# Down tiles of a SwiGLU beside attention: two steps in one group, and two PSUM banks as one tile

## The chip, the cores and the metric

The kernel runs on one core of a Trainium2 chip. The metric is the device time of one execution, in microseconds: the median of three runs of the kernel before is 1884.03 us (1881.98 to 1886.42). PE is TensorE, DVE VectorE, ACT ScalarE, POOL GpSimd, SP the queue that issues most DMAs.

## The reference

One transformer block on 2048 rows of width 512, in float32. There are 32 heads of 16 columns. The feed-forward width is 1792.

```
mod = silu(c) @ w_mod                      # shift, scale, gate, twice
h = layernorm(x) * (1 + ca) + sa
q, k, v = split(h @ wqkv);  p = softmax(q k^T / 4);  x = x + ga * ((p v) @ wo)
h = layernorm(x) * (1 + cb) + sb
x = x + gb * ((silu(h @ w_gate) * (h @ w_up)) @ w_down)
```

## The kernel before, in words

Float32 operands are split into a high part and a low part, and a product is three matmuls (high-high, high-low, low-high). Queries come in 4 chunks of 512 columns, heads in 8 groups of four, so attention is 32 units of 16 key tiles: 512 **steps**. A step is four **pairs**, one for each head of the group. One pair (`pair_of`, line 895) is

- a score matmul S (`score`, L506) with 50 of the 128 rows, and the exponential of its bank on ACT (L508);
- a max matmul M (`max_one`, L479) with 48 rows, of a step 20 steps ahead, and the row maximum of its bank on DVE (L481).

S and M sit in opposite row halves of the PE array and run at the same time. Every 16 steps `max_rows` adds three small matmuls (L491 to L493). PV matmuls (`pv_step`, L521) use all 128 rows and 32 columns each, and come in **halves**; each half is four matmuls in the program and eight records in the trace. They stand between runs of pairs.

PSUM has eight banks, and before the change each is a tile of its own. The order on PE is written out by hand in two kinds of stage:

- `plain` (line 928): **windows** of three pairs, then one or two PV halves (2, 1, 1, 2 in turn). M takes banks 0, 1, 2, 3 in turn, S takes 4, 5, 6 in turn. So every fourth M uses bank 3 and every third S uses bank 6. The row maximum sums in `max_rows` also take one turn of S's banks, so that after each 16 steps the bank 6 falls on another place in the window.
- `filled` (line 941): one **group** of two steps (`TWO`) or one step (`ONE`), with other matmuls put between its pairs (the numbers in the tuple say how many steps of that work follow each pair), and then its PV halves. M uses banks 0 to 2, S banks 4 and 5, and the work put in accumulates in banks 3 and 6 (`FBANKS`). The work is the output projection, the gate and up products (24 steps of two matmuls, in two `TWO` groups) or a **down tile** pair (12 steps of two matmuls, in two `ONE` groups).

The work put in goes through `accumulate` (line 709) in two **phases**: in phase 0 bank 3 sums products of rows 0 to 63 and bank 6 those of rows 64 to 127; in phase 1 they trade row halves. Before the change the two phases of a down tile lie in two groups, with PV matmuls of all 128 rows between them. After phase 1 DVE adds both banks to `x2` (L791).

After the last pair (about 1718 us) nothing is left of attention but its end, and `whole` runs the remaining 35 jobs on pairs of banks (0,1), (2,3), (4,5), (6,7) in turn, with all 128 rows (L727). Before the first pair, in the prologue, projections (L209) take banks 4 to 6, and the first 80 M take banks 0 to 3 beside them.

A matmul, a reduce or an exponential that needs a tile waits on the semaphore of the engine that used it last; the recording layer puts these waits in, tile by tile.

Of the kernel before, what the change touches and what calls it, by code (L numbers as in the profile page):

```python
# [9 lines left out]
F32 = mybir.dt.float32  # L10
# [9 lines left out]
P = 128  # L20
# [8 lines left out]
CW = S // NC  # L29
NG = H // 4  # L30
NU = NG * NC
NF = F // P
FG = 2
# [11 lines left out]
FBANKS = (3, 6)  # L45
# [2 lines left out]
NORM = 9  # L48
STARTS = (147, 275, 403)
TWO = (0, 3, 2, 2, 2, 2, 1, 0)  # L50
ONE = (0, 3, 3, 0)
ALONE = {TWO: ((0, 4, 0, 4, 0, 4, 0, 0), (4, 5, 0, 1, 5, 0, 4, 1)), ONE: ((0, 6, 0, 0), (4, 5, 4, 0))}


def run(it):
    for _ in it:
        pass


def take(it, k):  # L60
    run(islice(it, k))
# [40 lines left out]
def block_kernel(ctx, tc, x, wqkv, wo, w_gate, w_up, w_down, c, w_mod, out):  # L102
    nc = tc.nc
# [5 lines left out]
    ps = ctx.enter_context(tc.tile_pool(name="ps", bufs=1, space=PSUM))  # L109
    sm = Stream()  # L110

    banks = [ps.tile([P, CW], F32, name=f"bank{i}") for i in range(8)]

    class Turn:
        def __init__(self, *ids):
# [6 lines left out]
    four, bank, single = Turn(0, 1, 2, 3), Turn(4, 5, 6), Turn(7)  # L122
# [326 lines left out]
    pb = ctx.enter_context(tc.tile_pool(name="pb", bufs=2, reuse_waits="tile"))  # L449
# [7 lines left out]
    def ones_rows(k):  # L457
        for b in range(2):
            rows = slice(64 * b + KR, 64 * b + KR + 2)
            nc.sync.dma_start(kop[k][rows].bitcast(F32), kop[0][rows].bitcast(F32))  # L460

    def load_k(u):
        load_parts(kop[u % 3], kd, u % NG, 0, S, nc.gpsimd if u > 2 else nc.sync)

    def load_q(u):
        ci, g = divmod(u, NG)
        qop[u] = pb.tile([P, 2, CW], F32R, name="qop", tag="qop", bufs=3)
        load_parts(qop[u], qd, g, ci * CW, (ci + 1) * CW, nc.gpsimd if u > 2 else nc.sync)
# [14 lines left out]
    def max_rows(u):  # L483

        m = pb.tile([P, 16], F32, name="m", tag="m")
        nc.vector.tensor_reduce(m, mx.pop(u).rearrange("p b s t f -> p (b s t) f"), op=ALU.max, axis=AX.X)
        nm = pb.tile([P, 16], F32R, name="nm", tag="nm")

        def rows():
            pr = bank("pr")[0:16, 0:2 * P]  # L490
            nc.tensor.matmul(pr[:, 0:P], nm.bitcast(F32), ident, start=True, stop=True)  # L491
            nc.tensor.matmul(pr[:, P:2 * P], m, minus, start=True, stop=False)  # L492
            nc.tensor.matmul(pr[:, P:2 * P], nm.bitcast(F32), minus, start=False, stop=True)  # L493
            mr = pb.tile([16, 2, P], F32R, name="mr", tag="mr", bufs=1)
            nc.scalar.copy(mr, pr.rearrange("p (r q) -> p r q", r=2))
            for r in range(2):
                nc.sync.dma_start(qop[u][KR + r:KR + r + 65:64].bitcast(F32), mr[:, r, :].bitcast(F32))
        side.extend([lambda: None, lambda: None, lambda: nc.scalar.mul(nm, m, -1.0), lambda: None, rows])
# [207 lines left out]
            nc.gpsimd.tensor_copy(self.hT[0][:, k, :], h32)  # L706
            eng.tensor_sub(self.hT[1][:, k, :], h32, self.hT[0][:, k, :].bitcast(F32))

    def accumulate(outs, lhs, rhs, nk, after, halves, by_k=False):

        terms = [(k, a, b) for k in range(nk) for a, b in ((0, 0), (0, 1), (1, 0))]
        z = len(terms) - 1
        if halves:
            for ph in range(2):
                for j, (k, a, b) in enumerate(terms):
                    for e in range(2):
                        rows = slice(64 * (ph ^ e), 64 * (ph ^ e) + 64)
                        nc.tensor.matmul(outs[e], lhs(e, a, k)[rows], rhs(b, k)[rows],  # L718
                                         start=(ph == 0 and j == 0), stop=(ph == 1 and j == z))
                    if ph == 1 and j == z:  # L720
                        after()
                    yield
        else:
            order = [(e, j) for e in range(2) for j in range(z + 1)]
            for e, j in sorted(order, key=lambda o: o[1] // 3) if by_k else order:
                k, a, b = terms[j]
                nc.tensor.matmul(outs[e], lhs(e, a, k), rhs(b, k), start=(j == 0), stop=(j == z))  # L727
                if e == 1 and j == z:
                    after()
                yield  # L730
# [21 lines left out]
    def out_pair(ch, t0, outs, halves):  # L752
        return accumulate(outs, lambda e, a, k: ch.oT[a][:, k, (t0 + e) * P:(t0 + e + 1) * P],
                          lambda b, k: ch.wo[k // 2][:, b, k % 2, :], NK,
                          lambda: posts.append(lambda: add_o(ch, t0, outs, True)), halves)
# [31 lines left out]
    def down(ch, m, t0, outs, halves):  # L787
        def later():
            for e in range(2):
                t = t0 + e  # L790
                nc.vector.tensor_add(ch.x2[:, t, :], outs[e], ch.x2[:, t, :])  # L791
                if m == NF // FG - 1:
                    (nc.sync if ch.ci == last else nc.gpsimd).dma_start(od[:, 4 * ch.ci + t, :], ch.x2[:, t, :])

        def after():
            if halves:
                later()
            else:
                posts.append(later)
            if t0:  # L800
                ch.load_wd(m + 1)

        mids, wd = [ch.mid[FG * m + k] for k in range(FG)], ch.wd[m]
        return accumulate(outs, lambda e, a, k: mids[k][:, a, (t0 + e) * P:(t0 + e + 1) * P],
                          lambda b, k: wd[:, b, k, :], FG, after, halves, m == NF // FG - 1)

    chunks = {}
    side = []

    def begin(ci):  # L810
        x2 = pf.tile([P, 4, D], F32, name="x2", tag="x2", bufs=1)
        act = [pf.tile([P, NK, CW], F32R, name=f"act{a}", tag=f"act{a}", bufs=1) for a in range(2)]
        hT = [pf.tile([P, NK, CW], F32R, name=f"act{a}", tag=f"act{a}", bufs=1) for a in range(2)]
        chunks[ci] = ch = Chunk(ci, x2, act, hT)
        ch.load_x2(nc.sync if ci else nc.gpsimd)
# [8 lines left out]
    def hook():  # L824
        while posts:
            posts.pop(0)()
# [34 lines left out]
    def after(i):  # L861
        nonlocal pf
        for f in due.pop(i, []):
            f()
        j = i + LEAD
        if j % 16 == 15 and j < n:
            max_rows(j // 16)
        if i == -2:
            run(late)
            sm.finish()  # L870
            es_a0.close()
            pf = ctx.enter_context(tc.tile_pool(name="pf", bufs=1, side="right", reuse_waits="tile"))
            kop[2] = pf.tile([P, 2, S], F32R, name="kop2")
            ones_rows(2)
            load_k(2)
            load_q(2)
        if 0 <= i < UG and i % 16 in (3, 5, 8):
            next(weights2, None)
# [12 lines left out]
    halves = [(i, half) for i in range(n) for half in range(2)]  # L891
# [3 lines left out]
    def pair_of():  # L895
        nonlocal done
        i = done // 4 - 1
        most = 4 * n - 4 * (LEAD - 1)
        score(i + 1, (ORDER if done < most else (0, 1, 2, 3))[done % 4])
        if done < most:  # L900
            max_one(done + 4 * (LEAD - 1))
        done += 1
        if side:
            side.pop(0)()
# [17 lines left out]
    def end_steps():  # L922
        nonlocal ended
        while ended < done // 4:
            after(ended - 1)
            ended += 1
# [14 lines left out]
    def filled(places, work):  # L941

        nonlocal four, bank
        four, bank = three, Turn(4, 5)
        if done >= 4 * n - 4 * (LEAD - 1):
            places, order = ALONE.get(places, (places, (4, 5, 0, 1)))
            bank = Turn(*order)
        for r in range(len(places)):
            pair_of()
            take(work, places[r])  # L950
            if r % 4 == 3:
                end_steps()
        hook()
        pvs(6, False)
# [12 lines left out]
    outs = [banks[b] for b in FBANKS]  # L967
    for ci in range(last):
        plain(STARTS[ci] - done // 4)
        ch = chunks[ci]  # L970
        for t0 in (0, 2):
            work = out_pair(ch, t0, outs, True)
            filled(TWO, work)
            filled(TWO, work)
        side.append(lambda: scaled(ch))
        plain(NORM)
        plain(WIN, [lambda tp, k=k: ch.turned(tp, k) for k in range(NK)])
        if ci == last - 1:
            plain(REST)
        for _ in range(len(ch.jobs) - (KEEP if ci == last - 1 else 0)):  # L980
            job, args = ch.jobs.pop(0)
            if args == (NF // FG - 1, 0):
                plain(WIN)
            work = job(ch, *args, outs, True)
            for _ in range(2):
                filled(TWO if job is gate_up else ONE, work)
    chunks[last - 1].load_gu(NF - 2)
    filled((0,) * 4, iter(()))

# [70 lines left out]
```

## Time and profile before

| | |
|---|---|
| median of 3 runs | 1884.03 us |
| profiled execution: time, span | 1885.85 us, 1884.0 us |
| mean granted TensorE clock | 0.998 |
| PE, DVE, ACT, POOL busy | 99%, 82%, 66%, 22% of the span |
| chain of waits that ended last | PE 93%, DVE 3%, ACT 2%, DMA 2% |
| S and M | 2048 each (L506, L479), and as many exponentials and maxima |
| matmuls of the filled work | L718: 1872 + 288 of gate, up and output, 912 of down |

How to read it: a group row gives line, engine, operation, tiles and shapes, then the busy time, the mean ns of one, and the idle time of the engine before it. A row of the timeline begins with start and duration. A row of the windows view gives the stretch, its length, and the busy time of PE, PEld (weight loads), DVE, ACT and POOL with their counts. Bank numbers are left out of tile names. PE records overlap, since two row halves work at once, so PE's busy share says little of how full it is.

### The profile page before, as it was taken

The page shows a single profiled execution, that of the slowest core. Times are in us where ns is not written, and L with a number is a line of the kernel's source. Part 1 is how long each engine was busy: PE and PEld are TensorE (multiplying, and loading weights), DVE is VectorE, ACT ScalarE, POOL GpSimd, SP SyncE. Part 2 cuts the span into 40 slices and gives each one's busy share as a digit, 9 for nine tenths or more (in the row PEclk, how much of TensorE's full clock was granted, in tenths as well). Part 3 has the DMA queues.
Part 4 walks back from the last instruction along what each step waited for, and adds up shares of the span by engine and source line. Part 5 has one row for each costly group of instructions (what it writes and reads, how often), then busy time and mean ns, then how long its engine had stood idle before and what let it go on. Part 6 is the DMA issues. An engine that isn't in the chain of part 4 may idle for free.

```text
span 1884.0 us, 40835 instructions
## 1 busy us (share of the span) xinstructions
PE 1857.0 (99%) x16996; PEld 1145.3 (61%) x16996; DVE 1537.1 (82%) x2558; ACT 1249.8 (66%) x2330; POOL 414.6 (22%) x498
## 2 busy tenths in 40 slices
PE   7999999999999999999999999999999999999999
PEld 5766444444455666666555666666454566666887
DVE  5458999999999888888999888888999988831643
ACT  4221888888887766667777666667778866774211
POOL 3000554455323111111123111111123011031200
PEclk9999999999999999999999999999999999999999
DMA  8764777667843543554454453453643445243642
GB/s 297 279 213 124 178 182 196 181 172 184 209 85 78 140 110 117 141 128 88 112 118 114 105 137 116 127 121 78 153 91 55 102 98 128 107 160 122 243 184 109
DMA packets 78852, 267.60 MB, mean 142 GB/s; under 512 B 17364, under 2 KB 22484, under 8 KB 57988
## 3 DMA queue, kind: packets, MB, share of 16 engines
q1 hardware_dynamic: 59820, 180.10, 32.9%
q0 software_dynamic: 18160, 84.10, 19.0%
q8 instruction: 133, 2.18, 0.5%
q10 hardware_dynamic: 688, 0.80, 0.1%
q14 instruction: 51, 0.42, 0.1%
HBM read 201.85 MB, written 62.13 MB: 140 GB/s over the span
## 4 chain that ended last, share of the span: by engine, by line
PE 93%; DVE 3%; ACT 2%; DMA 2%; issue 0%; SPq 0%; ACTq 0%; DVEq 0%
PE bank L521 26%; PE bank L506 23%; PE bank L718 19%; PE bank L479 10%; PE bank L209 7%; PE bank L727 6%; DVE mx L481 1%; PE bank L491 1%; DVE stt L743 1%; PE bank L162 0%; PE bank L703 0%; DMA wm_ab<-in_w_mod 0%; PE bank L493 0%; PE bank L492 0%; PE bank L279 0%
## 5 line engine op out<-in xcount | busy, mean ns | idle before, releaser
L481 DVE TENSOR_REDUCE mx<-bank 128x1 f32<-128x512 f32 x2048 | 1282.9, 682 | 134.5 <-PE bank L479 86.5
L479 PE MATMUL bank<-kop,qop 48*128 48x512 f32 x2048 | 757.6, 434 | 3.3 <-DVE mx L481 3.1
L506 PE MATMUL bank<-qop,kop 50*128 50x512 f32 x2048 | 748.0, 429 | 3.3 <-DMA qop<-mr 0.5
L506 PEld LDWEIGHTS bank<-qop,kop 50*128 50x128 f32 x2048 | 344.5, 185 | 312.1 <-issue 48.1
L479 PEld LDWEIGHTS bank<-kop,qop 48*128 48x128 f32 x2048 | 342.4, 184 | 30.8 <-DVE mx L481 13.9
L718 PE MATMUL bank<-act,wgu 64*128 64x512 f32 x1872 | 296.6, 393 | 0.0
L718 PEld LDWEIGHTS bank<-act,wgu 64*128 64x128 f32 x1872 | 186.2, 187 | 31.4 <-issue 0.2
L548 POOL TENSOR_TENSOR on<-o,rb 128x512 f32<-128x512 f32 x31 | 39.7, 1281 | 450.7 <-DMA rb<-d_dr 299.1
L718 PE MATMUL bank<-wd,mid 64*128 64x512 f32 x912 | 130.8, 392 | 0.0
L779 POOL CAST mid<-m 128x512 fp32r<-128x512 f32 x40 | 24.3, 607 | 428.4 <-PE bank L479 175.4
L718 PEld LDWEIGHTS bank<-wd,mid 64*128 64x128 f32 x912 | 89.2, 186 | 15.2 <-issue 0.7
L209 PE MATMUL bank<-hT,wqs 128*128 128x512 f32 x384 | 95.8, 399 | 2.3 <-ACT hT L328 1.0
L209 PEld LDWEIGHTS bank<-hT,wqs 128*128 128x128 f32 x384 | 70.3, 188 | 24.4 <-issue 6.1
L775 DVE SCALAR_TENSOR_TENSOR q<-th,bank 128x512 f32<-128x512 f32 x56 | 37.7, 673 | 56.8 <-ACT th L771 56.8
L771 ACT ACTIVATE th<-bank 128x512 f32<-128x512 f32 x56 | 33.2, 594 | 58.5 <-PE bank L727 58.4
L791 DVE TENSOR_TENSOR x<-bank,x 128x512 f32<-128x512 f32 x84 | 53.9, 685 | 19.6 <-PE bank L718 19.6
L369 DVE TENSOR_TENSOR prt<-bank,prt 128x512 fp32r<-128x512 f32 x32 | 22.0, 688 | 46.2 <-ACT prt L367 43.9
L367 ACT CAST prt<-bank 128x512 fp32r<-128x512 f32 x32 | 18.8, 586 | 59.1 <-PE bank L209 47.1
L777 DVE TENSOR_TENSOR m<-bank,q 128x512 f32<-128x512 f32 x56 | 38.7, 691 | 21.2 <-PE bank L727 19.2
L727 PE MATMUL bank<-wd,mid 128*128 128x512 f32 x216 | 52.3, 395 | 0.5 <-DVE mid L780 0.3
L780 POOL TENSOR_TENSOR mid<-m,mid 128x512 fp32r<-128x512 f32 x40 | 51.6, 1289 | 3.3
L718 PE MATMUL bank<-wgu,act 64*128 64x512 f32 x288 | 47.7, 395 | 0.1
(6281 smaller groups left out, 5144.0 us busy)
## 6 DMA issues: line engine op xcount, KB each, us to landing
wgu<-gu_dr SPq DMA_DIRECT2D x48, 1024.0 KB
wd<-wd_dr SPq DMA_DIRECT2D x28, 1024.0 KB
kop<-kd SPq DMA_DIRECT2D x33, 768.0 KB
kop<-kd POOLq DMA_DIRECT2D x29, 768.0 KB, 8.5
gu_dr<-wgu POOLq DMA_DIRECT2D x14, 1024.0 KB, 14.3
kd<-prt SPq DMA_DIRECT2D x16, 512.0 KB
qd<-prt SPq DMA_DIRECT2D x16, 512.0 KB
kop<-gu_dr SPq DMA_DIRECT2D x8, 1024.0 KB
```

Of the source, the lines that this page charges most:

```text
L209: nc.tensor.matmul(pt, lhs(a, k), rhs(b, k), start=(n == 0), stop=(n == 3 * nk - 1))
L479: nc.tensor.matmul(pm, qop[u][rows, s, qt * P:(qt + 1) * P], kop[u % 3][rows, s, kc * CW:(kc + 1) * CW], start=True, stop=True)
L481: nc.vector.tensor_reduce(mx[u][:, b, s, qt, kc:kc + 1], pm, op=ALU.max, axis=AX.X)
L506: nc.tensor.matmul(sp, kop[u % 3][rows, h // 2, kt * P:(kt + 1) * P], qop[u][rows, h // 2, :], start=True, stop=True)
L521: nc.tensor.matmul(pv[u][32 * h:32 * h + 32, cols], v_flat[:, e0:e0 + 32], p_[h][:, cols], start=(kt == 0 and half == 0), stop=(kt == 15), ...
L548: mul.tensor_mul(on, o, rb)
L718: nc.tensor.matmul(outs[e], lhs(e, a, k)[rows], rhs(b, k)[rows], start=(ph == 0 and j == 0), stop=(ph == 1 and j == z))
L727: nc.tensor.matmul(outs[e], lhs(e, a, k), rhs(b, k), start=(j == 0), stop=(j == z))
L775: nc.vector.scalar_tensor_tensor(q, th, 1.0, outs[0], op0=ALU.add, op1=ALU.mult)
L777: nc.vector.tensor_mul(m32, outs[1], q)
L780: (nc.gpsimd if slow else nc.vector).tensor_sub(mid[:, 1, :], m32, mid[:, 0, :].bitcast(F32))
L791: nc.vector.tensor_add(ch.x2[:, t, :], outs[e], ch.x2[:, t, :])
```

## The change

Three things are changed.

1. `ONE`, a group of one step with three filled steps after pairs 1 and 2, is replaced by `DOWN`, a group of two steps: phase 0 after pairs 1 and 2, phase 1 after pairs 4 and 5, nothing after pairs 6 and 7. A down tile has one group now, and so one run of four PV halves in place of two runs of two. The table for the stage without M (`ALONE`) is changed to match.
2. Between the phases there are no PV matmuls any more. Instead ACT copies one element of both banks into a small tile `first` (`trade`), behind the last matmuls of phase 0, and the first matmul of phase 1 waits for that read.
3. To be read by one instruction, banks 3 and 6 become one tile `fpair` of two banks, and `banks[3]` and `banks[6]` are its two halves. All other users of these banks go through this tile too.

```diff
-ONE = (0, 3, 3, 0)
-ALONE = {TWO: ((0, 4, 0, 4, 0, 4, 0, 0), (4, 5, 0, 1, 5, 0, 4, 1)), ONE: ((0, 6, 0, 0), (4, 5, 4, 0))}
+DOWN = (0, 3, 3, 0, 3, 3, 0, 0)
+ALONE = {TWO: (0, 4, 0, 4, 0, 4, 0, 0), DOWN: (0, 6, 0, 0, 0, 6, 0, 0)}
...
-    banks = [ps.tile([P, CW], F32, name=f"bank{i}") for i in range(8)]
+    fpair = ps.tile([P, 2, CW], F32, name="fpair")
+    banks = [fpair[:, FBANKS.index(i), :] if i in FBANKS else ps.tile([P, CW], F32, name=f"bank{i}") for i in range(8)]
...
-    def accumulate(outs, lhs, rhs, nk, after, halves, by_k=False):
+    def accumulate(outs, lhs, rhs, nk, after, halves, by_k=False, trade=None):
...
-                                         start=(ph == 0 and j == 0), stop=(ph == 1 and j == z))
-                    if ph == 1 and j == z:
-                        after()
+                                         start=(ph == 0 and j == 0), stop=(j == z and (ph == 1 or trade is not None)),
+                                         skip_group_check=(ph == 1 and trade is not None))
+                    if j == z:
+                        (after if ph else trade or (lambda: None))()
...
-                          lambda b, k: wd[:, b, k, :], FG, after, halves, m == NF // FG - 1)
+                          lambda b, k: wd[:, b, k, :], FG, after, halves, m == NF // FG - 1,
+                          lambda: nc.scalar.copy(first[:, :, None], fpair[0:1, :, 0:1]))
...
+    first = pb.tile([1, 2], F32, name="first", bufs=1)
...
-            places, order = ALONE.get(places, (places, (4, 5, 0, 1)))
-            bank = Turn(*order)
+            places, bank = ALONE.get(places, places), Turn(4, 5, 0, 1, 5, 0, 4, 1)
...
-            for _ in range(2):
-                filled(TWO if job is gate_up else ONE, work)
+            for places in (TWO, TWO) if job is gate_up else (DOWN,):
+                filled(places, work)
```

**PE in a plain window.** The rows are in program order, with the engine whose semaphore each waits for; the lines are one higher after the change. In the names before, bank_63 to bank_70 are banks 0 to 7. After it fpair stands for banks 3 and 6, and bank_64, 65, 66, 67, 68, 69 are banks 0, 1, 2, 4, 5, 7. Before:

```order
L506 MATMUL bank_68<-qop,kop_961 128x512 [waits Activation_49]
L479 MATMUL bank_65<-kop_87,qop 128x512 [waits DMAHW7_49,DMAHW0_49,DVE_49]
L506 MATMUL bank_69<-qop,kop_961 128x512 [waits Activation_49]
L479 MATMUL bank_66<-kop_87,qop 128x512 [waits DVE_49]
L506 MATMUL bank_67<-qop,kop_961 128x512 [waits Activation_49]
L479 MATMUL bank_63<-kop_87,qop 128x512 [waits DVE_49]
L521 MATMUL bank_70<-pt__3750,v_flat 32x256
```

and the same place now:

```order
L507 MATMUL bank_68<-qop,kop_960 128x512 [waits Activation_49]
L480 MATMUL bank_66<-kop_86,qop 128x512 [waits DMAHW7_49,DMAHW0_49]
L507 MATMUL fpair<-qop,kop_960 128x512 [waits Activation_49]
L480 MATMUL fpair<-kop_86,qop 128x512 [waits Activation_49]
L507 MATMUL bank_67<-qop,kop_960 128x512
L480 MATMUL bank_64<-kop_86,qop 128x512 [waits DVE_49]
L522 MATMUL bank_69<-pt__3750,v_flat 32x256
```

No instruction moved here. The M on bank 3 (fourth row) waited for DVE and now waits for ACT; the count that it waits for is that of the exponential of the score in the row above it. In the window before this one stand an M and an S on fpair behind each other:

```order
L507 MATMUL bank_68<-qop,kop_960 128x512 [waits Activation_49]
L480 MATMUL fpair<-kop_1425,qop 128x512 [waits Activation_49]
L507 MATMUL fpair<-qop,kop_960 128x512 [waits DVE_49]
L480 MATMUL bank_64<-kop_86,qop 128x512 [waits DMASW3_49,DMASW2_49]
L507 MATMUL bank_67<-qop,kop_960 128x512 [waits Activation_49]
L480 MATMUL bank_65<-kop_86,qop 128x512
```

The S on bank 6, which waited for ACT before, waits for DVE here, and the count is that of the maximum of the M in the row above it. By the counts of the whole program, M on bank 3 waits in 78 cases for the exponential of its own pair, in 85 for that of the pair before and in 77 for that of two pairs before; S on bank 6 waits in 82 cases for the maximum of the pair before, in 77 for that of two and in 76 for that of three pairs before. Before the change there is not one such wait: M waited for the maximum four pairs back and S for the exponential three pairs back.

**PE in a down tile**, at the start of phase 1. Before, with the last three of the eight PV rows that stand between the phases:

```order
L521 MATMUL bank_70<-pt__8831,v_flat 32x256
L521 MATMUL bank_70<-pt__8822,v_flat 32x256
L521 MATMUL bank_70<-pt__8840,v_flat 32x256
L506 MATMUL bank_67<-qop,kop_961 128x512 [waits Activation_49]
L479 MATMUL bank_63<-kop_1425,qop 128x512 [waits DVE_49]
L506 MATMUL bank_68<-qop,kop_961 128x512 [waits Activation_49]
L479 MATMUL bank_64<-kop_1425,qop 128x512 [waits DVE_49]
L718 MATMUL bank_66<-wd,mid 128x512
```

and now, from the end of phase 0:

```order
L720 MATMUL fpair<-wd,mid 128x512
L507 MATMUL bank_68<-qop,kop_960 128x512 [waits Activation_49]
L480 MATMUL bank_66<-kop_1425,qop 128x512 [waits DVE_49]
L507 MATMUL bank_67<-qop,kop_960 128x512 [waits Activation_49]
L480 MATMUL bank_64<-kop_1425,qop 128x512 [waits DVE_49]
L720 MATMUL fpair<-wd,mid 128x512 [waits Activation_49]
L720 MATMUL fpair<-wd,mid 128x512 x5
L507 MATMUL bank_68<-qop,kop_960 128x512 [waits Activation_49]
```

The PV rows have left the middle of the tile, two pairs stand between the phases, and the first matmul of phase 1 waits for ACT, for the small copy. On ACT that copy stands between the exponentials of pairs 2 and 3:

```order
L509 ACTIVATE pt__8846<-bank_68 128x512 [waits PE_49]
L509 ACTIVATE pt__8875<-bank_67 128x512 [waits PE_49]
L509 ACTIVATE pt__8880<-bank_68 128x512 [waits PE_49]
L509 ACTIVATE pt__8891<-bank_67 128x512 [waits PE_49]
L809 COPY first<-fpair 1x2 [waits PE_49]
L509 ACTIVATE pt__8903<-bank_68 128x512 [waits PE_49]
```

Those are 38 new instructions on ACT, one for each down tile beside attention.

## The prediction

> **What bounds the kernel now.** I read the page's busy times first, then the windows view for the plain stages, then the timeline of single windows.
>
> ```profile
> PE 1857.0 (99%) x16996; PEld 1145.3 (61%) x16996; DVE 1537.1 (82%) x2558; ACT 1249.8 (66%) x2330; POOL 414.6 (22%) x498
> 192.00:546.50 354.50, 353.78 (x3532) 165.55 (x3524) 350.61 (x597) 307.31 (x606) 168.72 (x172) 1.00 0.69 178
> 404.55:411.70 7.15, 7.15 (x76) 3.36 (x72) 7.15 (x13) 6.19 (x12) 0.00 (x0) 1.00 0.96 345
> ```
>
> The first line makes PE the bound of the whole. The second is the longest plain stretch: there DVE is busy for 350.61 of 354.50 us, too. The third is one cycle of it, 12 pairs in four windows: 7.15 us, and DVE has no idle time in it. So a plain cycle costs 7.15 us, set by DVE, with PE's own work just beneath:
>
> ```profile
> 404.18 4.26 DVE L481 TENSOR_REDUCE mx<-bank 128x1 f32<-128x512 f32 x7
> 404.55 0.49 PE L506 MATMUL bank<-qop,kop 50*128 50x512 f32 x1
> 404.88 0.39 PE L506 MATMUL bank<-qop,kop 50*128 50x512 f32 x1
> 405.08 0.60 ACT L508 ACTIVATE pt__4169<-bank 128x512 f32<-128x512 f32 x1 [0.63 <-PE bank L479]
> 405.12 0.39 PE L506 MATMUL bank<-qop,kop 50*128 50x512 f32 x1
> 405.57 0.59 ACT L508 ACTIVATE pt__4174<-bank 128x512 f32<-128x512 f32 x1
> 406.05 0.61 ACT L508 ACTIVATE pt__4179<-bank 128x512 f32<-128x512 f32 x1
> 406.44 0.50 PE L506 MATMUL bank<-qop,kop 50*128 50x512 f32 x1
> 407.90 0.50 PE L506 MATMUL bank<-qop,kop 50*128 50x512 f32 x1
> ```
>
> In a window the three scores start at 0, 0.33 and 0.57 us (404.55, 404.88, 405.12). The next window starts 1.89 us after the first score with two PV halves (406.44) and 1.46 us with one (407.90). A cycle has two of each: 2 x 1.89 + 2 x 1.46 = 6.70 us of PE alone. The exponentials start 0.53, 1.02 and 1.50 us after the window's first score, since each follows the one before by 0.49. A maximum takes 4.26/7 = 0.61 in a row of seven; I use 0.60.
>
> **The change, first part: one tile for banks 3 and 6.** No instruction of a plain window moves, but M on bank 3 now waits for an exponential on bank 6, and S on bank 6 for a maximum on bank 3 (the waits of the built program, shown with the change). Such a wait stood nowhere before, so its price comes from single links of the chain where the engines were idle:
>
> ```profile
> 651.26 0.50 PE L506 MATMUL bank<-qop,kop 50*128 50x512 f32 x1
> 651.26 0.73 PE L479 MATMUL bank<-kop,qop 48*128 48x512 f32 x2
> 651.80 0.60 ACT L508 ACTIVATE pt__7287<-bank 128x512 f32<-128x512 f32 x1 [1.22 <-PE bank L506]
> 651.83 1.89 DVE L481 TENSOR_REDUCE mx<-bank 128x1 f32<-128x512 f32 x3 [0.18 <-PE bank L506]
> 652.45 0.18 PEld L506 LDWEIGHTS bank<-qop,kop 50*128 50x128 f32 x1 [0.19 <-ACT pt__7287 L508]
> 652.53 0.42 PE L506 MATMUL bank<-qop,kop 50*128 50x512 f32 x1
> ```
>
> An exponential ends at 652.40 and the matmul that waited for it starts at 652.53: 0.13. So a matmul that waits for the exponential of a window's first score can start 0.53 + 0.60 + 0.13 = 1.26 after that score, for the second score's 1.75 and for the third's 2.24. A maximum starts 0.57 after its M (651.26 to 651.83) and takes 0.68 (1.89 for three, pitch 0.60); with 0.10 for the release a waiting score starts 1.35 after a window's first M, and 1.95 if it is the second in DVE's queue. PE takes its matmuls in order, so all that stands behind the held one waits with it: the window's other pairs, its PV halves, and behind them ACT and DVE run empty.
>
> Number the pairs of a cycle 0 to 11; M on bank 3 is in pairs 3, 7 and 11. S on bank 6 stands on the first, second or third place of every window (the place moves by one each 16 steps). The holds are the price less the time at which PE would have come there by itself:
>
> - first place (pairs 0, 3, 6, 9): M3 waits for its own pair, 1.26; M7 for pair 6, 1.26 - 0.33 = 0.93; M11 for pair 9, 1.26 - 0.57 = 0.69; S of the next pair 0 for M11's maximum, 1.35 - (1.46 - 0.57) = 0.46. Sum 3.34.
> - second place: M3 for pair 1, over one PV half, 1.75 - 1.46 = 0.29; S4 for M3's maximum, 1.35 - 0.33 = 1.02; M7 for its own pair, 1.75 - 0.33 = 1.42; M11 for pair 10, 1.75 - 0.57 = 1.18. Sum 3.91.
> - third place: M3 for pair 2, 2.24 - 1.46 = 0.78; S5 for M3, 1.35 - 0.57 = 0.78; S8 for M7, 1.95 - 0.57 = 1.38; M11 for its own pair, 2.24 - 0.57 = 1.67. Sum 4.61.
>
> The mean is 3.95 on PE's own 6.70: 10.65 us a cycle, where DVE's 7.15 hid 0.45 of it: **+3.50**. Bounds: without any queue on ACT and DVE (every price 1.26 or 1.35, in-window holds alone) the places give 2.88, 3.11 and 3.06, mean 3.0, so 9.7 and +2.55; if all cycles were like the third place, 11.31 and +4.16. How many cycles: 240 M wait for ACT (78 + 85 + 77), three to a cycle, so 80. The page gives nearly the same:
>
> ```profile
> L718 PE MATMUL bank<-act,wgu 64*128 64x512 f32 x1872 | 296.6, 393 | 0.0
> L718 PE MATMUL bank<-wd,mid 64*128 64x512 f32 x912 | 130.8, 392 | 0.0
> L718 PE MATMUL bank<-wgu,act 64*128 64x512 f32 x288 | 47.7, 395 | 0.1
> ```
>
> (1872 + 288)/48 = 45 jobs of 16 pairs and 912/24 = 38 down tiles of 8 leave 2048 - 720 - 304 - 4 = 1020 pairs to plain windows, 85 cycles. I take 80: 80 x 3.50 = **+280 us**, between 80 x 2.55 = 204 and 85 x 4.16 = 354.
>
> The same tile joins the two banks in the prologue and the tail:
>
> ```profile
> 145.00:192.00 47.00, 45.72 (x205) 29.09 (x207) 41.57 (x69) 10.82 (x21) 3.18 (x4) 1.00 0.43 120
> L727 PE MATMUL bank<-wd,mid 128*128 128x512 f32 x216 | 52.3, 395 | 0.5 <-DVE mid L780 0.3
> L791 DVE TENSOR_TENSOR v_flat<-bank,v_flat 128x512 f32<-128x512 f32 x28 | 19.3, 689 | 10.6 <-PE bank L727 10.2
> ```
>
> In the prologue ten projection matmuls on bank 6 now wait for the fourth of four maxima in a row, up to 0.57 + 3 x 0.60 + 0.68 + 0.10 = 3.15 after the first M, of which the four M hide about 0.9. That is 22 us at most; DVE is idle for 5.4 of 47 us there, so part of the hold is work that DVE owes anyway. I take +12, bounds 3 and 22. In the tail a job on banks 6 and 7 follows one on 2 and 3 seven times, and must wait for the last add from bank 3: matmul 0.40, add 0.69, two releases 0.2, less a pitch of 0.2, so 1.1 each: +7, bounds 0 and 12. The small matmuls of `max_rows` no longer lie in DVE's shadow in plain stages: 0 to 14, I take +5.
>
> **Second part: one group in place of two.**
>
> ```profile
> 654.82:658.39 3.57, 3.57 (x42) 2.16 (x38) 3.00 (x5) 2.28 (x4) 0.00 (x0) 1.00 0.11 17
> 806.10:812.88 6.78, 6.78 (x78) 4.66 (x74) 5.65 (x9) 4.57 (x8) 3.04 (x4) 1.00 0.77 209
> L498 ACT ACTIVATE nm<-m x32: 207/216/232, 175.4 to 1660.9; 128x16 fp32r<-128x16 f32 x32
> ```
>
> The first stretch is a one-step group of a down tile with its PV run, the second a two-step group of a gate and up tile: it has just twice the matmuls of each kind. 2 x 3.57 - 6.78 = 0.36 is the price of one more passage between row halves and PV. 38 tiles x 0.36 = **-13.7**. DVE has 9 operations in the second stretch, 5.65 us; a down tile gives it ten (8 maxima, 2 adds), some 6.3, so it fits into 6.78.
>
> The trade costs ACT one small copy, nearest row 0.22. It starts when phase 0's last matmul has ended, 0.40 + 0.05 after its start; add 0.22 and 0.13, and phase 1 can start 0.80 after that matmul. Two pairs stand between, at the 0.24 of the window above (404.88 to 405.12), so PE comes there after 0.72: 0.08 a tile, 3 us for 38. Behind the copy ACT has the exponential of pair 3, which only the score of pair 5 needs. The bounds are 0 and 0.35, if the copy queues behind half an exponential (13 us): I take +3. Together -11, between -14 and 0. The cover of the copy is those two pairs; without them it would cost 0.80 - 0.24 = 0.56 a tile, 21 us.
>
> **Sum**: 280 + 12 + 7 + 5 - 11 = +293 on the profiled span of 1884.0 us: 2177. That execution took 1885.85, 1.85 more than its span, and the median of the three runs is 1884.03, as good as the span; I forecast **2177 us**. The bounds added are 1884 + 204 + 3 - 14 = 2077 and 1884 + 354 + 22 + 12 + 14 + 0 = 2286, all unlikely at once.
>
> **The rivals.**
>
> *The new waits stand on work that has ended* (not slower). Then the plain cycle stays at 7.15 and only the second part is left: 1884 - 11 = **1873**. For it speaks that holds over two PV halves are nil in my list, since 1.26 is less than 1.89. Against it: the M that waits for its own pair's exponential cannot be early, as that exponential starts 0.53 after the score beside it. It decides from the point where the prices fall below the gap of 0 to 0.6 us; no row shows an exponential that short. The Trainium skill, page "PSUM — Partial Sum Buffer", section "Specifications (TRN2)", says that ScalarE and VectorE can read PSUM in parallel at full bandwidth as long as there is no bank collision. By that rule banks 3 and 6 need no order between them, and the chip would give the 1873; the rows of the built program have the waits all the same. Chance 0.05.
>
> *One hold a cycle*: a hold lets ACT and DVE catch up, and the others vanish in its shadow. Then a cycle is 6.70 + 1.45 (mean of 1.26, 1.42 and 1.67) = 8.15, +1.0 x 80: with the other terms **1977**. Against it: each hold is measured from a score or M that itself comes after the earlier hold. Chance 0.07.
>
> *The granted clock falls* where PE stops three or four times in 10 us. It is 1.00 in the windows rows above. At half clock PE's own 6.70 would double at most, +536; over half the plain time **2445**. Against it: no hold is longer than 1.7 us. Chance 0.05. The skill's page "TensorE: Matmul & The Clock Gate", section "A second HAM failure mode: psum-queue depth-cycling", tells of a kernel that cycled through PSUM banks, with micro-idle times between groups of matmuls, and whose clock swung between half and full. No run here shows that yet.
>
> **How the numbers follow.** My forecast has 0.83, the rivals 0.05, 0.07 and 0.05. The likeliest case's own range is 2090 to 2250: the two bounds drawn in, since its terms do not all err one way. It holds most of the 0.83, and what is left out is about 2 in 10, so it is the range. 0.2% of 1884 is 3.8 us, which is what a measurement can tell from no change; only the first rival could be faster (0.04) or the same (0.02, with a dearer trade). Slower 0.94.
>
> **What would show it.** Right: in the same plain stretch a cycle of 10 to 11.5 us, DVE some 67% busy in it (7.15 of 10.65), PE's idle time before L480 released by the exponentials (L509) and before L507 by the maxima (L481), some 235 times each, in the first case 1.2 to 1.7 long for M of the own pair; down tiles at 6.7 to 6.9 us a group; clock still 1.00. Wrong: a plain cycle of 7.2, or holds before L480 of 0.3 and less; a clock below 1; or 38 long waits on the small copy (L809).

## The result, and the profile after

The changed kernel takes **2429.26 us** in the median (six runs, 2421.35 to 2471.52), the kernel before 1884.68 us in the runs beside it: a ratio of **1.288** (95% interval 1.285 to 1.291; the medians themselves give 1.289). The forecast was 2177 us, range 2090 to 2250: the direction was right, and 252 us are missing. The profiled execution of the changed kernel is its slowest, 2471.52 us at a mean clock of 0.837, where the other five have 0.854 to 0.867, so its stages are read below by clock, and the ratios here and below leave out executions more than 1.5% above the fastest of the same kernel.

From the page of the changed kernel, the busy times, the granted clock in 40 slices, and the chain of waits by engine:

```profile
PE 2225.3 (90%) x16996; PEld 1254.6 (51%) x16996; DVE 1589.2 (64%) x2558; ACT 1280.4 (52%) x2368; POOL 415.0 (17%) x498
PEclk9987559675765797999995989999857768999999
PE 83%; DVE 8%; ACT 8%; issue 1%; DMA 0%; SPq 0%; ACTq 0%; DVEq 0%
```

DVE fell from 82% to 64% of a longer span, and DVE and ACT entered the chain with 8% each, from 3% and 2%. That is the theory of holds. But the second line was not foreseen: the clock, 1.00 before, goes down to half for whole slices. The windows view of the changed kernel (columns as before, granted clock third from the end), for the longest plain stretch, a part of it at full clock, a part at half clock, and the tail:

```profile
219.20:890.30 671.10, 574.16 (x3549) 228.12 (x3549) 382.50 (x604) 327.24 (x614) 171.51 (x176) 0.66 0.37 96
374.00:446.00 72.00, 57.28 (x502) 24.65 (x498) 53.55 (x85) 46.58 (x88) 31.65 (x35) 1.00 0.53 135
265.00:370.00 105.00, 91.88 (x479) 34.94 (x478) 51.10 (x81) 43.16 (x81) 20.30 (x21) 0.50 0.26 70
2298.00:2469.00 171.00, 161.78 (x722) 128.10 (x720) 69.50 (x117) 27.38 (x45) 10.96 (x14) 1.00 0.44 169
```

The second row has DVE busy for 53.55 of 72.00 us (0.74); the third does about as much work (81 maxima and exponentials against 85 and 88) in 105 us. Counting the scores that start at each clock in the longest plain stretch of 587 pairs: 241 pairs in 213.7 us at full clock, **10.64 us for a cycle of 12**, and 346 pairs in 457.4 us at half clock, **15.86 us**. Before, the same count gives 7.30 (the 7.15 of a bare cycle, and the small matmuls of `max_rows`).

By stage, from the times of the first and last scores: the prologue ends at 219.2 us (187.4 before, +31.8), the longest plain stretch takes 671.1 (358.8, +312.3), the rest beside attention 1407.7 (1171.8, +235.9), the tail 171.7 (166.0, +5.7). Together +585.7 us in this execution.

### The profile page after: what moved, and what is told of

It reads as the page before. It is cut to its first block, busy times and chain, and to the rows that moved or that the text cites. A ratio compares the mean times of both kernels' runs of the same rounds, so it can differ in the third digit from the quotient of the medians.

```text
span 2469.7 us, 41150 instructions
## 1 busy us (share of the span) xinstructions
PE 2225.3 (90%) x16996; PEld 1254.6 (51%) x16996; DVE 1589.2 (64%) x2558; ACT 1280.4 (52%) x2368; POOL 415.0 (17%) x498
## 4 chain that ended last, share of the span: by engine, by line
PE 83%; DVE 8%; ACT 8%; issue 1%; DMA 0%; SPq 0%; ACTq 0%; DVEq 0%
PE bank L522 25%; PE bank L507 15%; PE fpair L720 14%; DVE mx L482 7%; PE bank L480 6%; PE fpair L507 4%; PE bank L730 4%; PE fpair L480 4%; PE bank L210 3%; PE fpair L210 2%; PE fpair L730 1%; PE fpair L704 0%; PE bank L763 0%; PE bank L492 0%; DVE stt L746 0%
## 5 line engine op out<-in xcount | busy, mean ns | idle before, releaser
L482 DVE TENSOR_REDUCE mx<-bank 128x1 f32<-128x512 f32 x1782 | 1162.6, 687 | 503.5 <-PE bank L480 428.6
L720 PE MATMUL fpair<-act,wgu 64*128 64x512 f32 x1872 | 296.3, 392 | 0.0
L482 DVE TENSOR_REDUCE mx<-fpair 128x1 f32<-128x512 f32 x266 | 183.2, 689 | 151.5 <-PE fpair L480 88.4
L507 PE MATMUL fpair<-qop,kop 50*128 50x512 f32 x334 | 197.7, 592 | 83.4 <-DVE mx L482 83.0
L480 PE MATMUL fpair<-kop,qop 48*128 48x512 f32 x266 | 166.0, 624 | 98.1 <-ACT pt__1682 L509 1.2
L720 PEld LDWEIGHTS fpair<-act,wgu 64*128 64x128 f32 x1872 | 183.3, 187 | 34.4 <-DVE m L780 3.1
L507 PEld LDWEIGHTS fpair<-qop,kop 50*128 50x128 f32 x334 | 84.3, 252 | 181.5 <-DVE mx L482 160.0
L480 PEld LDWEIGHTS fpair<-kop,qop 48*128 48x128 f32 x266 | 64.2, 241 | 182.4 <-ACT pt__5971 L509 1.6
L720 PE MATMUL fpair<-wd,mid 64*128 64x512 f32 x912 | 134.3, 397 | 0.0
L720 PEld LDWEIGHTS fpair<-wd,mid 64*128 64x128 f32 x912 | 86.1, 186 | 16.9 <-issue 3.1
```

The source lines that it names most:

```text
L480: nc.tensor.matmul(pm, qop[u][rows, s, qt * P:(qt + 1) * P], kop[u % 3][rows, s, kc * CW:(kc + 1) * CW], start=True, stop=True)
L482: nc.vector.tensor_reduce(mx[u][:, b, s, qt, kc:kc + 1], pm, op=ALU.max, axis=AX.X)
L507: nc.tensor.matmul(sp, kop[u % 3][rows, h // 2, kt * P:(kt + 1) * P], qop[u][rows, h // 2, :], start=True, stop=True)
```

## The experiments

**The holds themselves**, in the timeline of the changed kernel (start, duration, work, then the idle time before it and what ended it):

```profile
388.52 0.50 PE L507 MATMUL fpair<-qop,kop 50*128 50x512 f32 x1
389.05 0.60 ACT L509 ACTIVATE pt__2484<-fpair 128x512 f32<-128x512 f32 x1 [0.52 <-PE fpair L507]
389.70 0.49 PE L480 MATMUL fpair<-kop,qop 48*128 48x512 f32 x1 [0.45 <-ACT pt__2484 L509]
392.55 0.49 PE L480 MATMUL fpair<-kop,qop 48*128 48x512 f32 x1 [0.22 <-ACT pt__2507 L509]
393.14 0.68 DVE L482 TENSOR_REDUCE mx<-fpair 128x1 f32<-128x512 f32 x1
393.88 0.50 PE L507 MATMUL fpair<-qop,kop 50*128 50x512 f32 x1 [0.26 <-DVE mx L482]
```

An M on bank 3 starts 1.18 us after the score on bank 6 (388.52 to 389.70), behind its exponential; a score on bank 6 starts 1.33 us after the M on bank 3 (392.55 to 393.88), behind its maximum. The prices in the forecast were 1.26 and 1.35. In the longest plain stretch at full clock, 33 of the 56 M on bank 3 start 1.18 or 1.19 us after the last score on bank 6; the others come later. In the page's groups, the idle time before these two kinds of matmul, and before their weight loads:

```profile
L507 PE MATMUL fpair<-qop,kop 50*128 50x512 f32 x334 | 197.7, 592 | 83.4 <-DVE mx L482 83.0
L480 PE MATMUL fpair<-kop,qop 48*128 48x512 f32 x266 | 166.0, 624 | 98.1 <-ACT pt__1682 L509 1.2
L507 PEld LDWEIGHTS fpair<-qop,kop 50*128 50x128 f32 x334 | 84.3, 252 | 181.5 <-DVE mx L482 160.0
L480 PEld LDWEIGHTS fpair<-kop,qop 48*128 48x128 f32 x266 | 64.2, 241 | 182.4 <-ACT pt__5971 L509 1.6
```

Scores on fpair wait for maxima, M on fpair for exponentials, as the order of waits said. (Each exponential has a name of its own, so the last column shows only the longest of many.)

### The shared tile alone

The kernel before, with nothing but banks 3 and 6 made one tile:

```diff
-    banks = [ps.tile([P, CW], F32, name=f"bank{i}") for i in range(8)]
+    fpair = ps.tile([P, 2, CW], F32, name="fpair")
+    banks = [fpair[:, FBANKS.index(i), :] if i in FBANKS else ps.tile([P, CW], F32, name=f"bank{i}") for i in range(8)]
```

> The kernel before with nothing changed but banks 3 and 6 as one tile; down tiles keep their two one-step groups, and there is no trade. Theory: as slow as the changed kernel, plus the 11 us that the joined groups saved there: 2415 to 2465 us, clock 0.84 to 0.88. Rival (the groups and the trade carry the loss): 1884 us, clock 1.00.

Measured: 2436.21 us, ratio 1.292 (1.287 to 1.297). The windows row of its longest plain stretch:

```profile
216.70:843.30 626.60, 523.01 (x3550) 211.90 (x3549) 381.57 (x605) 325.39 (x614) 171.31 (x176) 0.74 0.39 103
```

Its cycle is 10.67 us at full clock (344 pairs) and 15.84 at half clock (243). The whole loss is in the tile, half clock included.

### The change without the shared tile

The changed kernel with eight separate bank tiles; the trade is two ACT copies, one of each bank.

```diff
+    banks = [ps.tile([P, CW], F32, name=f"bank{i}") for i in range(8)]
...
+                          lambda: [nc.scalar.copy(first[:, e:e + 1], outs[e][0:1, 0:1]) for e in range(2)])
```

> The two-step down groups and the trade stay, banks 3 and 6 are tiles of their own again, and the trade is two small ScalarE copies, one from each bank. Theory (the joined tile is the whole loss): the plain cycle is back at 7.15 us, the granted clock at 1.00, and the time is 1884 less 10 for the 38 joined groups: 1868 to 1880 us. Rival (the groups or the trade cost time themselves, by the copies that hold phase 1): 1890 us or more, with waits of the first L720 of phase 1 on the copies of over 0.4 us each.

Measured: **1879.07 us, ratio 0.9969 (0.9958 to 0.9981)**: the idea of one group of two steps is worth about 6 us (the runs of the kernel before beside these have a median of 1885.23). Its windows view, one down tile beside M, and one after the last M:

```profile
651.09:657.93 6.84, 6.84 (x74) 4.71 (x72) 6.40 (x11) 4.97 (x12) 1.90 (x2) 1.00 0.74 109
1661.02:1667.80 6.78, 6.27 (x66) 4.11 (x66) 1.44 (x3) 4.85 (x12) 3.71 (x5) 1.00 0.18 35
```

Beside M, 6.84 against 2 x 3.57. But the second row has PE busy for 6.27 of 6.78 us only, and the two groups that it replaces took 3.04 to 3.06 each, some 6.1 together. One of them, in the windows view of the kernel before:

```profile
1672.04:1675.10 3.06, 3.06 (x34) 1.84 (x32) 0.13 (x1) 2.17 (x4) 1.64 (x3) 1.00 0.52 125
```

The changed kernel has the same pair of numbers, and the small copy in it costs little (durations are min, median, max in ns, and below who waited for it, in us and times):

```profile
1019.24:1026.08 6.84, 6.84 (x74) 4.50 (x72) 6.38 (x11) 4.89 (x11) 1.90 (x2) 1.00 0.78 113
2245.11:2251.89 6.78, 6.27 (x65) 4.00 (x64) 1.43 (x3) 4.55 (x11) 3.72 (x5) 1.00 0.21 47
...
L809 ACT COPY first<-fpair x38: 150/151/153, 1023.5 to 2292.6; 1x2 f32<-1x2 f32 x38
  PE fpair L720: 3.7, 19
```

### The stage without M

There are four such down tiles. In the timeline of the kernel with separate tiles, a score there waits for an exponential that stands behind the copies:

```profile
1664.79 0.20 ACT L808 COPY first<-bank 1x1 f32<-1x1 f32 x2 [0.29 <-PE bank L719]
1665.09 0.60 ACT L508 ACTIVATE pt__20063<-bank 128x512 f32<-128x512 f32 x1
1665.74 0.49 PE L506 MATMUL bank<-qop,kop 50*128 50x512 f32 x1 [0.51 <-ACT pt__20063 L508]
```

The order of banks for S there, `4, 5, 0, 1, 5, 0, 4, 1`, comes back to a bank after two pairs at the group's edge and after three inside. Bank 2 is free in this stage. With it a bank comes back after five pairs inside, three at the edge:

```diff
-            places, bank = ALONE.get(places, places), Turn(4, 5, 0, 1, 5, 0, 4, 1)
+            order = (4, 5, 0, 1, 2, 4, 5, 0) if places == DOWN else (4, 5, 0, 1, 5, 0, 4, 1)
+            places, bank = ALONE.get(places, places), Turn(*order)
```

> As the run with separate tiles and the trade by two small copies, but the four down tiles after the last M take their scores' banks in the order 4, 5, 0, 1, 2, 4, 5, 0 in place of 4, 5, 0, 1, 5, 0, 4, 1, so that the fifth score does not wait for the exponential of the second. In the run with separate tiles these four groups took 6.70 to 6.78 us each, where two one-step groups before took 6.10; the other 34 tiles took 6.87 in place of 7.12. Theory (that bank order is what the groups lose there): the four groups take 6.2 us or less, 2 us in all: 1876 to 1878 us. Rival (the trade itself is what they lose, since phase 1 has little to stand behind there): no change, 1879 us.

Measured: **1875.47 us, ratio 0.9947 (0.9934 to 0.9961)**, faster than the kernel before and the changed one, and half a microsecond below what was expected. The same down tile:

```profile
1661.53:1667.38 5.85, 5.85 (x66) 4.15 (x65) 1.49 (x3) 4.56 (x11) 3.67 (x5) 1.00 0.10 13
```

6.78 went to 5.85, and PE has no idle time in it. The four tiles took 6.78, 6.71, 6.77 and 6.70 us, and take 5.85, 5.95, 5.85 and 5.93 now: 3.4 us less in all, where the medians differ by 3.6.

### The cross waits taken out of plain windows

The changed kernel with M on banks 0 to 2 in plain windows, so that only S uses the shared tile there:

```diff
-        four, bank = Turn(0, 1, 2, 3), Turn(4, 5, 6)
+        four, bank = Turn(0, 1, 2), Turn(4, 5, 6)
```

> The changed kernel, with M in plain windows on banks 0, 1, 2 alone; the joined tile and the trade's single read stay, and bank 3 has no user in a plain window. Theory: no wait crosses from S to M there, so no hold of 0.7 to 1.7 us and clock 1.00 after the prologue; M waits for the maximum three pairs back instead of four, which costs 0 to 0.2 us a window: 1880 to 1950 us. Rival (a tile of two banks is slow by itself, whoever uses it): above 2100 us.

Measured: 1959.57 us, ratio 1.039 (1.038 to 1.041), 10 us above what was expected. The longest plain stretch:

```profile
214.90:597.90 383.00, 382.13 (x3549) 192.73 (x3549) 362.78 (x604) 315.48 (x614) 171.97 (x176) 0.99 0.64 167
```

The cycle is 7.74 us and the clock 0.99. So 470 of 545 us hang on the waits between banks 3 and 6 in plain windows. Of the other 75, some 37 are plain cycles of 7.74 in place of 7.30 (85 x 0.44; M has three banks there in place of four) and 27.5 the prologue (its end is at 214.9); the tail and what remains were not split further.

### A hold of another kind

Is it the shared tile that lowers the clock, or any hold? The kernel before, separate tiles, but S on two banks in plain windows, so that a score waits for the exponential two pairs back:

```diff
-        four, bank = Turn(0, 1, 2, 3), Turn(4, 5, 6)
+        four, bank = Turn(0, 1, 2, 3), Turn(4, 5)
```

> The kernel before with separate tiles, but S in plain windows on banks 4 and 5 alone. No tile is joined; each third score of a window waits for the exponential of the first, a hold of 0.53 + 0.60 + 0.13 - 0.57 = 0.69 in every window. Theory A: a cycle of 6.70 + 4 x 0.69 = 9.46 us, 85 of them at +2.31: 2080 us (2050 to 2120), and since the holds are even and the array is used a tenth more than in the changed kernel, clock 0.98 or more. Theory B (clock falls with the number of holds): some 340 holds like the 470 of the changed kernel, clock under 0.93 and 2200 us or more.

Measured: 2200.57 us in the median of four (2170.64 to 2223.08), ratio 1.157 (1.152 to 1.163).

```profile
189.50:740.00 550.50, 472.69 (x3551) 185.16 (x3550) 377.98 (x606) 338.22 (x615) 171.42 (x176) 0.81 0.44 117
```

At full clock a cycle takes 9.66 us (9.46 expected from the prices of the forecast), but 166 of 587 pairs ran at half clock, 15.3 us a cycle. The time missed its range by the clock: the profiled execution (2206 us) has some 345 us at half clock, which cost 1 - 9.66/15.3 of themselves, 127 us; without them it would be near 2080. So the clock falls without a shared tile, too.

### More work beside the holds

If the clock falls because PE does too little in a stretch, work that no one needs should hold it up. First, each plain M that isn't on bank 3 is issued twice:

```diff
+        for _ in range(1 if pm is banks[3] else times[0]):   # times[0] = 2 in plain
```

> The changed kernel, with each M of a plain window issued twice onto its bank, except those on bank 3: nine matmuls more in a 12-pair cycle, same results. The waits across the joined tile stay. Theory A (the clock is halved when too small a share of a few microseconds is streamed): the share in a full-clock cycle rises from about 24 x 0.217 / 10.65 = 0.49 to 0.6, so the clock is 0.95 or more, and the time falls although PE has more to do: a cycle of 11 to 12 us, 2190 to 2310 us. Theory B (the clock falls with the stops themselves, whatever is done between them): clock 0.87 or less as in the changed kernel, and 2480 us or more.

Measured: 2486.78 us in the median (2437 to 2527; clock 0.864 to 0.912), so the clock of 0.95 or more and the time that go with PE's share of time (theory A) are not there. The time is that of theory B; its clock, 0.87 or less, only one of the four executions has. The longest plain stretch:

```profile
216.50:885.50 669.00, 575.46 (x3990) 264.40 (x3990) 384.00 (x605) 332.41 (x614) 171.49 (x176) 0.78 0.36 97
```

It has 3990 matmul records in place of 3549, but a third of the pairs (197 of 587) still ran at half clock, where the changed kernel had 346 and the shared tile alone 243; the cycle at full clock became 11.55 us. An M fills 48 of 128 rows, so this adds little work. Second, one float32 matmul of 128 rows and 512 columns ahead of each M on bank 3, where most of these M would wait anyway:

```diff
+        if pm is banks[3] and fill[0]:                      # in plain
+            nc.tensor.matmul(banks[0], ident, v_flat[:, 0:CW], start=True, stop=True)
```

> The changed kernel, with one float32 matmul of the identity with 512 columns of v put ahead of each M on bank 3 in plain windows, onto bank 0, whose next M overwrites it; about 0.85 us of all 128 rows at a place where PE stands still for 0.7 to 1.7 us. All waits across the joined tile stay. Theory A (the clock is halved when the array is used too little in a window of 3.41 us, by rows and columns and not by time alone): used share of a full-clock cycle up by about 3 x 0.85 / 10.7 = 0.24, clock 0.96 or more, and a cycle of 10.7 to 11.4 us at full clock: 2170 to 2260 us, some 200 us faster than the changed kernel with 250 matmuls more. Theory B (the waits between engines bring the clock down, whatever is put into them): clock 0.88 or less, 2430 us or more.

Measured: 2392.33 us (2369.09 to 2424.98), clock 0.964 to 0.992. Third, the same with 64 rows, in the row half of the next M:

```diff
+            n_ = 64 * (1 - (r + 1) % 4 // 2)
+            nc.tensor.matmul(banks[0], ident[n_:n_ + 64], v_flat[n_:n_ + 64, 0:CW], start=True, stop=True)
```

> The changed kernel with one float32 matmul of 64 rows and 512 columns (into bank 0, whose next M overwrites it) ahead of each M on bank 3 in plain stages, in place of the filler of 128 rows: about half the added work, and no change of row mode beside the scores. Theory A, the clock follows the share of the array that is used, and falls under about 0.35: the filler lifts the share of a plain cycle from 0.26 to 0.34 to some 0.38 to 0.45, so the clock is 0.96 or more, the cycle at full clock 10.7 to 11.5 us (10.64 in the changed kernel), the time 2170 to 2290 us: the predicted 2177 or a little above. Theory B, the clock follows the stops themselves, however much runs between them: the clock stays at 0.93 or less and the time at 2330 us or more.

Measured: 2308.53 us (2302.7 to 2313.55), ratio 1.225 (1.222 to 1.227), clock 0.973 to 0.980. The longest plain stretch with 128 rows, then with 64 rows, with the group of that filler:

```profile
215.60:824.70 609.10, 567.41 (x3841) 222.66 (x3841) 384.96 (x604) 323.86 (x613) 171.48 (x176) 1.00 0.40 106
...
216.80:771.10 554.30, 505.34 (x3841) 224.94 (x3841) 385.11 (x604) 323.94 (x614) 171.60 (x176) 1.00 0.44 117
L485 PE MATMUL bank<-v_flat,ident 64*128 64x512 f32 x492 | 258.2, 605 | 0.0
```

In both **no part of the stretch is at half clock**, with all cross waits in place, where the changed kernel had 457 us of it. Work that is thrown away made the kernel 121 us faster. The cycles are longer, 12.45 and 11.33 us in place of 10.64; the second lies inside what was expected, the first a whole us above it, and both times missed their ranges on the high side. A filler of 64 rows takes about 1 us (two records), and the holds of M on bank 3 are 0.29 to 1.67 in the forecast's list; so it is longer than some of them (and 71 of the 246 fillers start behind the M on bank 3 in the trace). That this is the whole of the 0.69 was not measured. In the 64-row kernel 108 us at half clock are left, some 20 in the prologue and nearly all the rest in the shorter plain stretches.

The fillers do two things at once: they use more of the array, and they fill the stops. At full clock PE stands still for 22% of the longest plain stretch in the changed kernel, 19% with M issued twice and 19% with S on two banks, but for 7% and 9% with the two fillers. So these runs show that work in the holds keeps the clock up; they do not tell the used share from the stops. The last section looks at single stretches for that.

## Why the prediction was wrong in size

**The failed step is the clock.** The forecast had it at 1.00, and put "The granted clock falls" among the rivals with a chance of 0.05 and 2445 us, against it the sentence "no hold is longer than 1.7 us". The premise nearly holds: inside the plain stretches of the changed kernel PE stood still for at most 1.3 us at a time in the 8 us before a fall (stops of 2.3 to 2.4 us stand before four falls in the prologue and before three just behind the steps from filled to plain stages). The conclusion does not: before the other falls beside attention the longest stop is 0.6 to 1.3 us. Half-clock time in the profiled execution is 807.6 us in 27 pieces. In the longest plain stretch it cost 457.4 x (1 - 10.64/15.86) = 151 us, in the rest beside attention there are 317 us at half clock, nearly all in plain stretches, and at the same rate they cost 104. At the clock of the median runs (0.864, so 2 x 0.136 x 2429 = 661 us at half clock) it is some 220 us of the 252 that were missed, if all of it costs a third. That the rival's own figure, 2445, is near is luck in part: it took half of the plain time without a row for that half, and the price of a doubled PE pitch.

**The term of the holds was right.** 10.65 us a cycle was forecast from 7.15; 10.64 was measured at full clock, small matmuls of `max_rows` included, from 7.30. With 85 cycles that is 85 x 3.34 = 284 us, where 280 + 5 stood; that the two agree to 1 us is luck in part, since 80 cycles at 3.50 stood for 85 at 3.34. The two prices are 1.18 and 1.33 for 1.26 and 1.35. The three places of bank 6 can be told apart, too: whole cycles at full clock, without the small matmuls, take 9.97 us with S on bank 6 in the first place (29 cycles), 10.82 in the second (6) and 11.30 in the third (4), where 10.04, 10.61 and 11.31 follow from the list of holds. The rival of one hold a cycle (8.15) and that of waits on ended work (7.15) are out.

**Prologue and tail.** +12 was taken for the prologue, bounds 3 and 22; it grew by 31.8. In the waits of the changed kernel (us in total, times, longest):

```profile
PE fpair L210 <- DVE mx L482: 17.6, 9, 2.4
PE fpair L730 <- DVE v_flat L794: 4.7, 6, 0.8
```

The first row is the projections on bank 6 behind maxima: nine of the ten holds that were listed, nearer the upper bound than the middle; why less of their time lay over other work is not shown. Half clock for 31 us between 133 and 205 us adds at most 15, probably the part that took the prologue beyond its upper bound. The second row is the tail: +5.7 measured, +7 forecast.

**One group in place of two.** Beside M the sum had 0.36 less for the passage and 0.08 more for the trade, 0.28 a tile; measured are 0.2 to 0.3 (34 groups, medians 6.88 and 6.91 with and without the shared tile, where two groups took 7.14). The trade's waits are 3.7 us in all; 3 was taken. What was missed is that four of the 38 tiles run without M. They were costed like the others and lost 0.65 each by the order of banks for S. Together 34 x (-0.23) + 4 x 0.65 = -5.2 us, where -11 stood; the kernel with separate tiles shows about -6.

**The sum again**, for the profiled execution: 284 for the holds, 151 + 104 for the clock in plain windows, 32 for the prologue, 6 for the tail, -5 for the groups: 572 of 585.7 us. The other 14 are not placed. Without the clock the sum is about 1884 + 284 + 17 to 32 + 6 - 5, 2186 to 2201 us, inside the range forecast.

The Trainium skill, page "PSUM — Partial Sum Buffer", section "Specifications (TRN2)", says that ScalarE and VectorE can read PSUM in parallel at full bandwidth as long as no bank collides. The rival that named it had 1873. The kernel with separate tiles, at 1879.07, is what the rule leaves where the program does not tie the banks together; with the shared tile the waits are in the program, and the rule has nothing to decide.

## What to carry to other kernels

A tile is the unit in which a program waits: two banks in one tile are one bank to every engine that touches either, so before joining buffers for one small instruction, list all their other users and price the new waits (here two tiny reads of separate tiles in place of one read of a joined tile do the same, and are 550 us faster). Price such holds by single links of the chain, and then ask a second question: how much of the PE array the stretch still uses with the holds in it, for in the runs here the clock halved where that was too little, and every estimate made at full clock was off. And where one stage of a loop lacks a partner (here M), cost its groups from their own rows.

## What the runs showed of the hardware

**The clock follows the used share of the array more closely than the stops.** The granted clock changes only in steps of 3.41 us, between 1.00 and 0.50. For each such stretch I added up, over the matmul records, columns moved x 0.42 ns (twice that at half clock) x rows/128 x output columns/128, and divided by 3.41 us. Records with float32 operands count twice: those of PV, 256 columns wide, follow each other on the same tile at 0.21 to 0.22 us, as long as 512 columns take at 0.42 ns. (The 0.42 is half of what a column takes at half clock: in the prologue of the changed kernel projections of 512 columns follow each other at 0.427 us there, 0.83 ns a column.) In the timeline of the changed kernel:

```profile
387.76 0.38 PE L522 MATMUL bank<-pt__2401,v_flat 128*32 128x256 f32 x1
387.97 0.38 PE L522 MATMUL bank<-pt__2401,v_flat 128*32 128x256 f32 x1
388.19 0.38 PE L522 MATMUL bank<-pt__2401,v_flat 128*32 128x256 f32 x1
```

Over the ten profiled executions (both kernels and all eight experiments), by the share of one stretch and the clock of the next:

| share in a stretch at full clock | next at full | next at half |
|---|---|---|
| below 0.30 | 5 | 60 |
| 0.30 to 0.38 | 45 | 69 |
| 0.38 to 0.42 | 190 | 4 |
| 0.42 and more | 5185 | 0 |

| share in a stretch at half clock | next at half | next at full |
|---|---|---|
| below 0.70 | 609 | 22 |
| 0.70 to 0.75 | 75 | 59 |
| 0.75 and more | 3 | 62 |

So it falls below about 0.38 and comes back above about 0.72 (at half clock the same work fills a larger share). In the longest plain stretch, at full clock, from 220 us on (the step into the stretch is left out; single falls stand there in several kernels, the kernel before among them):

| kernel | mean share | stretches below 0.38 | falls |
|---|---|---|---|
| before; separate tiles | 0.62; 0.62 | 0 of 94; 0 of 95 | 0; 0 |
| M on banks 0 to 2 | 0.58 | 0 of 108 | 0 |
| 128-row filler; 64-row filler | 0.57; 0.51 | 1 of 175; 1 of 160 | 0; 0 |
| S on two banks | 0.46 | 18 of 90 | 8 |
| M issued twice | 0.45 | 11 of 109 | 8 |
| changed kernel; shared tile alone | 0.42; 0.42 | 12 of 61; 19 of 89 | 9; 10 |

The changed kernel's windows with long holds dip under the lower limit, and once at half clock its mean share is 0.58, under the upper one: it stays there until some window is denser, up to 109 us. The spread of the changed kernel's times by 2% goes with this: 2421.35 us at a mean clock of 0.867, 2471.52 at 0.837. The limits fit the failure of the doubled M (0.45, 11 stretches too low) and the success of the fillers, but so do the stops of these kernels. Single stretches tell the two apart better. Among those at full clock in which at least one matmul was moving columns for 45 to 60% of the time, 49 of 86 with a share below 0.38 were followed by a fall, and 3 of 463 with a higher share. And of 28 stretches with a stop of over 1 us, but a share of 0.42 or more, none was. This is a sorting of what happened, not an experiment that varied one and held the other. The limits are read off these ten executions after the fact; only the last run was made with a limit in mind, 0.35 by a count that did not yet double float32 records.

The Trainium skill, page "TensorE: Matmul & The Clock Gate", section "What's actually happening", says that the clock is halved after at least one idle window of about 3.4 us. The 3.41 us agree. That the window must be idle does not: of the stretches in which 0.30 to 0.38 of the array was in use, 69 of 114 were followed by half clock here. The section "A second HAM failure mode: psum-queue depth-cycling", which the rival named, describes what these runs show, frequent short stops and a clock that swings.
